# Decode of the second block's weights begun four groups later, the coarse score's third part taken first, and one y operand shifted, in a fused attention and two-block kernel

## The chip, the cores and the metric

The kernel runs on one core of one Trainium2 chip. The metric is the device time of one execution in microseconds, from the chip's own records; lower is better. A change of about 0.5% (4 us) is the least that the measurement of this kernel tells from no change.

## The reference

`setup_inputs` draws 4 batches of 8 heads, 576 positions of 64 elements, all float32. Each head gets two attentions that are added: a coarse one over means of 4 positions (144 by 144 scores), repeated 4 times, and a local one with a band of 7 positions. The sum, as 2304 tokens by 512, goes through two blocks of products.

```python
out_d = sm_attn(q_d, k_d, v_d)            # q, k, v averaged over 4 positions: 144 x 144 scores
out_up = np.repeat(out_d, factor, axis=2)
mask = np.abs(pos[:, None] - pos[None, :]) < factor
...
return (out_up + out_local).astype(np.float32)

def _moe_ref(x, w1, w2, w3, w_out):       # 512 -> 1024 -> 512
    a = x @ w1
    b = x @ w2
    h = a * b @ w3
    return (h @ w_out).astype(np.float32)

def _moe2_ref(x, w_in, w_out):            # 512 -> 2048 -> 512
    h = x @ w_in
    g = h * (1.0 / (1.0 + np.exp(-h)))
    return (g @ w_out).astype(np.float32)
```

## The kernel before

**Work and stages.** One pass over the core's time has four stages. An opening (to about 109 us) loads and decodes the first block's weights and runs the first attention units by a list of names written out by hand. Then come the `ab` products (x by w1 and w2, line 675), 128 *groups* numbered by slot; then the `yb` products (line 1126, from 360 us), the second block's first product `h` (line 1180) and its second `o` (line 1313). Weights arrive as 64-bit numbers and are turned into float32 on the chip: ScalarE scales (line 186, `dec`), VectorE clamps (line 191), shifts the low word (line 197, `sw`) and joins (line 203).

**Order.** From slot 18 on, TensorE's order is fixed by the code; the other engines' orders are set by a scheduler that simulates the program, so that an edit of a start slot moves rows on all of them. Every engine runs its rows in order. So does SP, whose queue issues every DMA, and a DMA that waits holds up those behind it.

**Attention in the background.** The 16 *units* (two heads each) run beside the `ab` groups. TensorE counts a *beat* after every three matmuls (four to a group), and the tables `SUMS` and `TURN` name the beat of each step of a unit u: `td` (transposes of the coarse scores, line 439) and `tl` (of the local ones, line 469), `od` (coarse sums, line 499), `sd` of the next unit (its coarse scores, lines 372 and 377), `s` (its local scores, line 414), and `ol` (local sums, line 521). From `sd` to `ol` lie 8 beats for the pairs 7/6 and 8/7 (`sd7` to `ol6`, `sd8` to `ol7`), and 14 for later ones. After `sd`, VectorE takes maxima (lines 396 and 398, `smd`), a mean of the next unit's q and k (line 321, `qkd`) and the scaled maxima (line 399); ScalarE then takes exponentials (line 339, `Ed` from `sd`, then `band`), GpSimd normalizes (line 356). The result of `ol` goes out as `xf` (VectorE, line 534), a ScalarE cast (line 549) and GpSimd's rest (line 553) to `x`, which the `ab` products of the next batch read.

**Two T banks.** `od`, the third part of a split coarse score (`sd_1`, `other` in the code), both halves of `ol`, `td` and `tl` share two PSUM tiles of tag T, in rotation. The second half of `ol` takes the one that held `sd_1`, so it waits until the exponentials have read the third part. A score is split for units over 5.

**Decode in the background.** `units` of the second block's weights (16, line 760) are loaded by `bg_load` (two DMAs of 512 KB into one of two staging buffers, `sw`), and `bg_steps` puts their decode and four mixes (line 814, `res`) and stores at slots from `starts[n]`:

```python
starts = [22 + (13 * n) // 3 for n in range(len(units))]
at(NSTATIC + 2, lambda: bg_load(0))       # NSTATIC is 18
...
(0, first), (1, clamp), (3, low), (4, lambda: bg_load(n + 2)),
(4, lambda: mix(0)), (5, store_plain), (5, lambda: mix(1)), (6, store_mixed),
```

At `bg_end` = `starts[-1] + 9` the pools of the next stage open and `r_load(0)` reads four blocks of the `ab` results back (`cb`, `cr`, line 960).

**y operands.** Seven tiles of tag `c_` (6 KB a partition) hold the split operands of the `yb` and `h` products, in rotation. After the `h` stage, tiles of the `o` stage (A, S1 to S4) lie where they were.

Of the kernel before, what the change touches and what calls it, by code (L numbers as in the profile page):

```python
# [9 lines left out]
F32R = mybir.dt.float32r  # L10
AF = mybir.ActivationFunctionType
ALU = mybir.AluOpType
AX = mybir.AxisListType

NB, NHP, S, P = 4, 4, 576, 128
# [4 lines left out]
NQB, QW, KW = 9, 32, 38  # L20
# [53 lines left out]
def tile_model(ctx: ExitStack, tc: tile.TileContext, qk, vw, vr, w12, w3t, wo, wb, out):  # L74
    nc = tc.nc
# [69 lines left out]
    for g in range(4):  # L145
        mv = mask[QW * g:QW * g + QW]
        nc.gpsimd.affine_select(
            out=mv, in_=mv, compare_op=ALU.is_ge, fill=NEG, base=0,
# [3 lines left out]
            out=mv, in_=mv, compare_op=ALU.is_ge, fill=NEG, base=6,  # L152
# [13 lines left out]
    def op(name, fn):  # L166
        assert name not in ops, name
        ops[name] = fn
# [11 lines left out]
    def stage(home, name):  # L180
        return home.tile([P, 2, 512, 2], I32, tag="st", name=name, bufs=2)
# [148 lines left out]
    def unit_ops(u):  # L330
        U = str(u)
        hold = {}
# [1 line left out]
        def small(tag):  # L334
            return att.tile([P, 2 * NQB], F32, tag=tag, name=tag)

        def exps(z, src, E, lo, hi, n, scale):
            for j in range(lo, hi):
                nc.scalar.activation(  # L339
                    E[:, j, :], src[j], AF.Exp, bias=z[:, j:j + 1], scale=scale,  # L340
                    accum_out=z[:, NQB + j:NQB + j + 1],
                )
# [8 lines left out]
        def norm(z, E, n, width, lo, hi):  # L351
            if opening[0]:
                for j in range(lo, hi):
                    nc.scalar.mul(E[:, j, :], E[:, j, :], z[:, NQB + j:NQB + j + 1])
            elif lo == 0:
                nc.gpsimd.tensor_tensor(
                    out=E, in0=E, op=ALU.mult,
                    in1=z[:, NQB:NQB + n].unsqueeze(2).to_broadcast([P, n, width]),
                )

        split = u > 5
# [30 lines left out]
        def coarse_max():  # L392
            hold["zd"] = att.tile([P, NQB + 3], F32, tag="smd", name="smd")
            m = hold["zd"][:, 3:6]
            n = 2 if split else 3
            nc.vector.tensor_reduce(out=m[:, :n], in_=hold["pair"], axis=AX.X, op=ALU.max)
            if split:
                nc.vector.tensor_reduce(out=m[:, 2:3], in_=hold["sv"][2], axis=AX.X, op=ALU.max)
            nc.vector.tensor_scalar(
                out=hold["zd"][:, 0:3], in0=m, scalar1=-1.0 / 128.0, scalar2=None, op0=ALU.mult  # L400
            )

        def coarse_exps():
            hold["Ed"] = att.tile([P, 3, SD], F32, tag="Ed", name=f"Ed{u}", bufs=1)
            exps(hold["zd"], hold["sv"], hold["Ed"], 0, 3, 3, 1.0 / 128.0)

        def local_scores():
            t = A["qk", u]
# [12 lines left out]
        EL = band[:, :, 0:KW]  # L421
# [40 lines left out]
        def local_turn(k):  # L462
            c0, c1, w = TL[k]
            flat = band.rearrange("p i k -> p (i k)")
            if k == 0:
                hold["ET"] = att.tile([64 + KW, 5, P], F32, tag="ET", name=f"ET{u}", bufs=1)
            tp = t_tile(f"tl{u}_{c0}")
            for c in range(c0, c1):
                nc.tensor.transpose(
                    tp[:w, (c - c0) * P:(c - c0 + 1) * P], flat[:, 128 * c:128 * c + w], ident,  # L470
                )
            hold["tl", k] = tp

        def local_copy(k):
            c0, c1, w = TL[k]
            mark(nc.scalar.copy(
                hold["ET"][:w, c0:c1, :].rearrange("p c q -> p (c q)"),
                hold["tl", k][:w, :(c1 - c0) * P],
            ))
# [83 lines left out]
        op("mk" + U, local_mask)  # L563
        op("ml" + U, local_max)
        for k in range(3):
            op(f"x{k}" + U, lambda k=k: exps(hold["zl"], [EL[:, j, :] for j in range(NQB)], EL, 3 * k, 3 * k + 3, NQB, 1.0))
            op(f"n{k}" + U, lambda k=k: norm(hold["zl"], EL, NQB, KW, 3 * k, 3 * k + 3))
            op(f"tl{k}" + U, lambda k=k: local_turn(k))
            op(f"cl{k}" + U, lambda k=k: local_copy(k))
# [18 lines left out]
    for u in range(NU):  # L588
        unit_ops(u)
# [71 lines left out]
    NH = 384  # L661
    NT = NTOK // (2 * NH)
# [80 lines left out]
    NSTATIC = 18  # L743
# [16 lines left out]
    units = [(kind, p) for p in range(8) for kind in range(2)]  # L760
    bg = {}

    def bg_load(n):
        if n >= len(units):
            return
        kind, p = units[n]
        if wide:
            st = stage(stg, "sw")
        else:
            st = stg.tile([P, 2, 512], F32, tag="st", name="sw", bufs=2)  # L770
        for t in range(2):
            src = wb[2 * p + kind, :, t * 512:(t + 1) * 512]
            if wide:
                nc.sync.dma_start(st[:, t].rearrange("p n w -> p (n w)"), src.bitcast(I32))
            else:
                nc.sync.dma_start(st[:, t], src)
        bg["st", n] = st
# [57 lines left out]
    def at(slot, fn):  # L835
        plan.setdefault(slot, []).append(fn)

    starts = [22 + (13 * n) // 3 for n in range(len(units))]
    at(NSTATIC + 2, lambda: bg_load(0))
    at(NSTATIC + 5, lambda: bg_load(1))  # L840
    for n in range(len(units)):
        for k, fn in bg_steps(n):
            at(starts[n] + k, fn)
# [1 line left out]

    NUN = 8 * NT
    yp = []
    Y, YC, WC = {}, {}, {}


# [23 lines left out]
    def cx_half(name, dtype):  # L874
        return b3[0].tile([P, 4 * NH], dtype, tag="ch", name=name, bufs=2)

    def y_high(t, i, e=None):
        if i // 2 == 2 * t - 2 and t:
            d = cx_half(f"yc{t}_{i}", F32R).rearrange("p (l k n) -> p l k n", l=2, k=2)
        elif t == 1 and 2 <= i < 4:  # L880
            d = b2[0].tile([P, 2, 8 * P], F32R, tag="a", name=f"yc{t}_{i}", bufs=2)
            d = d[:, :, :2 * NH].rearrange("p l (k n) -> p l k n", k=2)
        else:
            d = yp[0].tile([P, 2, 2, NH], F32R, tag="c_", name=f"yc{t}_{i}", bufs=7)
        if e is None:
            nc.scalar.copy(d[:, 0], Y[t][CH[i][0]])
        else:
            e.tensor_copy(d[:, 0], Y[t][CH[i][0]])
        YC[t, i] = d
# [89 lines left out]
    def r_slot(j, g):  # L979
        name = f"co{j}_{g}"  # L980
        if j == 20:
            return cx_half(name, F32R).rearrange("p (l k n) -> p l k n", l=2, k=2)
        if j == 19 or (j < 14 and (2 * j + g) % 9 > 6):
            d = b2[0].tile([P, 2, 8 * P], F32R, tag="a", name=name, bufs=2)
            return d[:, :, :2 * NH].rearrange("p l (k n) -> p l k n", k=2)
        return yp[0].tile([P, 2, 2, NH], F32R, tag="c_", name=name, bufs=7)

    def r_split(j, g):
        t, i = divmod(j, 7)
# [13 lines left out]
    def w_mix(name):  # L1003
        q = {
            "q0": WQ[0][:, 0], "q3": WQ[0][:, 1], "q1": WQ[1][:, 0], "q2": WQ[1][:, 1],
        }
        if name == "r2":
            v = c_pools[0].tile([P, 4, 256], F32, tag="rw", name="rw", bufs=1)
            nc.vector.tensor_tensor(out=v, in0=q["q3"], in1=q["q2"], op=ALU.add)
            WY["f", 5] = v  # L1010
        elif name == "r3":
            nc.vector.tensor_tensor(out=q["q3"], in0=q["q0"], in1=q["q3"], op=ALU.subtract)
            WY["f", 6] = q["q3"]
        elif name == "r0":
            v = WY["f", 5]
            nc.vector.tensor_tensor(out=v, in0=v, in1=q["q0"], op=ALU.subtract)
            WY["f", 3] = v
        else:
            nc.vector.tensor_tensor(out=q["q1"], in0=q["q1"], in1=WY["f", 3], op=ALU.subtract)
            WY["f", 4] = q["q1"]  # L1020

    def w_split(o):
# [9 lines left out]
    todo = (  # L1032
        (102, lambda: w_mix("r2")), (104, lambda: w_mix("r3")),
        (105, lambda: r_split(0, 0)), (105, lambda: r_split(0, 1)),
        (106, lambda: r_mix(0, "t1")), (107, lambda: r_split(1, 0)), (108, lambda: r_split(1, 1)),
        (110, lambda: r_split(2, 0)), (111, lambda: r_split(2, 1)), (112, lambda: r_mix(0, "t2")),
        (113, lambda: r_split(3, 0)),
        (101, lambda: w_split(0)), (105, lambda: w_split(5)), (107, lambda: w_mix("r0")),
        (109, lambda: w_split(1)), (114, lambda: w_split(3)), (115, lambda: w_mix("r1")),
        (117, lambda: w_split(2)), (121, lambda: w_split(4)), (125, lambda: w_split(6)),  # L1040
# [358 lines left out]
    E = mybir.EngineType  # L1399
    with tc.manual_schedule(engines={E.PE, E.DVE, E.Activation, E.Pool, E.SP}):  # L1400
        for t in range(NT):
# [10 lines left out]
            for i in range(7):  # L1412
                j = 7 * t + i
# [18 lines left out]
        for u in range(NUN):  # L1432
            t, p = divmod(u, 8)
# [5 lines left out]
            if t == 0:  # L1439
                todo = {p_: (2 * p_ + 2, 2 * p_ + 3) for p_ in range(6)}  # L1440
                for k, s in enumerate(todo.get(p, ())):
                    put((1, 3)[k], lambda s=s: wc_high(s), lambda s=s: wc_rest(s, nc.vector))
            if t + 1 < NT:
# [4 lines left out]
                todo = {5: ((4, 0),), 6: ((1, 1), (3, 2), (5, 3)), 7: ((1, 4), (3, 5), (5, 6))}  # L1448
# [83 lines left out]
```

## Time and profile before

| | |
|---|---|
| median of 3 runs | 805.39 us (805.06, 805.39, 808.16) |
| profiled execution, its own time | 804.82 us |
| span in the profile | 803.0 us |
| PE, PEld busy | 99%, 92% of the span |
| DVE, ACT, POOL busy | 71%, 56%, 8% |
| mean granted TensorE clock | 0.997 |

PE is TensorE's matmuls, PEld its weight loads, DVE VectorE, ACT ScalarE, POOL GpSimd, SPq the SP queue that issues DMAs. Busy shares are of the span from first to last instruction; the execution's own time is 1.8 us longer. A granted clock of 1.0 is 2.4 GHz, 0.5 is 1.2 GHz.

### The profile page before, as it was taken

The numbers are of one execution on the slowest core, as the hardware profiler recorded it, in microseconds if no ns is written. First come the engines' busy times: TensorE is split into PE (matmuls) and PEld (weight loads), VectorE is DVE, ScalarE is ACT, GpSimd is POOL, SyncE is SP. The second block draws the span as 40 slices with busy tenths as digits, with TensorE's granted clock in tenths as the row PEclk, the third lists the DMA queues.
The fourth block names the chain that finished last, engine by engine and source line by source line (L and its number), as shares of the span: only waits on it lengthen the run. The fifth ranks groups of instructions, "written<-read, shape, count | busy, mean of one in ns | idle before, by whom it ended". The sixth has DMA issues, their size and how long they took to land.

```text
span 803.0 us, 19022 instructions
## 1 busy us (share of the span) xinstructions
PE 791.6 (99%) x7510; PEld 739.7 (92%) x7510; DVE 569.4 (71%) x870; ACT 445.8 (56%) x1136; POOL 67.5 (8%) x84
## 2 busy tenths in 40 slices
PE   8999999999999999999999999999999999999998
PEld 5555699889999999999999999999999999999998
DVE  7988884867878874836889567445565798777771
ACT  6687864555555552525447577547578654444441
POOL 3000101423332220000000000000000000000000
PEclk9999999999999999999999999999999999999999
DMA  9977774689899887226485663454788955555540
GB/s 312 379 213 250 237 230 136 182 248 297 289 304 312 273 279 257 52 49 235 132 321 152 203 197 99 123 177 115 239 257 239 334 184 190 185 187 185 192 132 27
DMA packets 109353, 168.68 MB, mean 210 GB/s; under 512 B 20176, under 2 KB 80080, under 8 KB 108880
## 3 DMA queue, kind: packets, MB, share of 16 engines
q1 hardware_dynamic: 109264, 167.46, 65.0%
q8 instruction: 59, 0.97, 0.5%
q14 instruction: 30, 0.25, 0.1%
HBM read 115.00 MB, written 52.43 MB: 209 GB/s over the span
## 4 chain that ended last, share of the span: by engine, by line
PE 87%; DMA 5%; DVE 4%; issue 1%; SPq 1%; ACT 1%; POOL 0%; DVEq 0%; ACTq 0%; POOLq 0%
PE ab L675 23%; PE yb L1126 11%; PE ox L1313 10%; PE hx L1180 9%; PE oy L1313 6%; PE hy L1180 6%; PE wp L635 3%; PE oz L1313 3%; PE hv L1180 3%; PE hz L1180 3%; PE ov L1313 3%; PE ol L521 2%; DMA st<-w 2%; DMA vr<-vr 1%; DMA qk<-qk 1%; PE td L439 1%
## 5 line engine op out<-in xcount | busy, mean ns | idle before, releaser
L675 PE MATMUL ab<-x,w_wB 128*128 128x320 f32 (+1 forms) x768 | 109.6, 300 | 0.0
L675 PE MATMUL ab<-x,w_wA 128*128 128x320 f32 (+1 forms) x768 | 107.6, 297 | 1.0 <-DVE w_wA L280 1.0
L675 PEld LDWEIGHTS ab<-x,w_wB 128*128 128x128 f32 x768 | 103.7, 190 | 1.1 <-issue 0.7
L675 PEld LDWEIGHTS ab<-x,w_wA 128*128 128x128 f32 x768 | 102.2, 189 | 1.8 <-DVE w_wA L280 1.3
L1126 PE MATMUL yb<-co,wy 128*128 128x384 f32 x504 | 87.5, 336 | 0.0
L1126 PEld LDWEIGHTS yb<-co,wy 128*128 128x128 f32 x504 | 87.3, 188 | 0.0
L1180 PE MATMUL hx<-yc,wc 128*128 128x384 f32 x432 | 82.9, 336 | 0.0
L1180 PEld LDWEIGHTS hx<-yc,wc 128*128 128x128 f32 x432 | 75.6, 188 | 0.0
L635 PE MATMUL wp<-w_wo,w_w 128*128 128x512 f32 x128 | 60.1, 602 | 0.3 <-DVE w_wo L203 0.2
L1180 PE MATMUL hy<-yc,wc 128*128 128x384 f32 x288 | 57.8, 336 | 0.0
L687 ACT COPY af<-ab 128x320 f32<-128x320 f32 (+1 forms) x64 | 25.1, 396 | 58.5 <-PE ab L675 52.2
L1313 PE MATMUL oy<-wo,S 128*128 128x256 f32 x432 | 53.8, 281 | 0.0
L1313 PE MATMUL ox<-wo,S 128*128 128x256 f32 x432 | 53.8, 281 | 0.0
L1313 PEld LDWEIGHTS oy<-wo,S 128*128 128x128 f32 x432 | 52.2, 189 | 0.0
L1313 PEld LDWEIGHTS ox<-wo,S 128*128 128x128 f32 x432 | 52.2, 189 | 0.0
L1180 PEld LDWEIGHTS hy<-yc,wc 128*128 128x128 f32 x288 | 50.6, 188 | 0.0
L1162 ACT ACTIVATE c<-c 128x384 f32<-128x384 f32 x96 | 48.0, 525 | 3.8 <-DVE c L1092 3.1
L693 DVE TENSOR_TENSOR cf<-ab,af 128x320 f32<-128x320 f32 (+1 forms) x64 | 28.8, 449 | 24.8 <-PE ab L675 11.4
L339 ACT ACTIVATE band<-band,sml 128x38 f32<-128x38 f32 x144 | 44.9, 319 | 2.2 <-DVE sml L430 2.2
L635 PEld LDWEIGHTS wp<-w_wo,w_w 128*128 128x128 f32 x128 | 22.4, 190 | 21.2 <-issue 19.0
L1186 ACT COPY p<-hx 128x384 f32<-128x384 f32 x24 | 11.5, 478 | 44.4 <-PE hx L1180 44.4
L993 DVE TENSOR_TENSOR co<-cb,co 128x768 fp32r<-128x768 f32 x32 | 29.3, 955 | 9.3 <-ACT co L992 8.6
(183 smaller groups left out, 1455.5 us busy)
## 6 DMA issues: line engine op xcount, KB each, us to landing
gd<-c SPq DMA_DIRECT2D x96, 192.0 KB
sw<-wb SPq DMA_DIRECT2D x32, 512.0 KB
qk<-qk SPq DMA_DIRECT2D x16, 579.0 KB
big<-gd SPq DMA_DIRECT2D x18, 512.0 KB
A<-gd SPq DMA_DIRECT2D x18, 512.0 KB
S<-gd SPq DMA_DIRECT2D x17, 512.0 KB
cb<-cd SPq DMA_DIRECT2D x10, 768.0 KB
st<-w SPq DMA_DIRECT2D x14, 512.0 KB
```

The lines of the kernel that those rows point to most:

```text
L339: nc.scalar.activation(E[:, j, :], src[j], AF.Exp, bias=z[:, j:j + 1], scale=scale, accum_out=z[:, NQB + j:NQB + j + 1],)
L521: nc.tensor.matmul(acc[h][r, c0:c0 + QW], lhsT=v[k, sub, c, r], rhs=ET[k, c, q0:q0 + QW], start=True, stop=True,)
L635: nc.tensor.matmul(wp_ps[half, j], lhsT=w3v[:, k, j * P:(j + 1) * P], rhs=wov[:, k, :], start=(gp == 0 and k == 0), stop=(gp == 3 and k == 1),
L675: nc.tensor.matmul(acc[:, :N], lhsT=wv[:, i, w, kk, :], rhs=X[b, h, kk][:, j, :], start=(n == 0), stop=(n == 11),)
L687: mark(nc.scalar.copy(af, C.pop(("ab", b, h, m, 0))[:, :N]))
L693: nc.vector.tensor_tensor(out=cf, in0=C.pop(("ab", b, h, m, 1))[:, :N], in1=C.pop(("af", b, h, m)), op=ALU.mult)
L993: nc.vector.tensor_tensor(out=d[:, 1], in0=src, in1=d[:, 0].bitcast(F32), op=ALU.subtract)
L1126: nc.tensor.matmul(acc[e], lhsT=WY[o][:, a, 2 * g + k, c0:c0 + P], rhs=y[:, b, k, :], start=(n < 2 and (a, b) == (0, 0) and i in (0, 1, 2, ...
L1162: nc.scalar.activation(v, v, AF.Silu)
L1180: nc.tensor.matmul(acc, lhsT=WC[s][:, a, c, kt * P:(kt + 1) * P], rhs=y[:, b, kt, :], start=(n == 0 and i in (0, 1, 2, 4)), stop=(n == 5), ...
L1186: nc.scalar.copy(p1, X_)
L1313: nc.tensor.matmul(acc, lhsT=A[:, a, p * P:(p + 1) * P], rhs=B_[name, p // 4][:, b, p % 4, :], start=(p == 0 and q == 0 and name in begin) ...
```

## The change

Three edits. The background decode starts at slot 26 and steps by 17/4 slots a unit (before: 22 and 13/3), and its first two loads are asked for 3 slots later. For split scores the maximum and the exponential of the third part come first. The tag `c_` becomes seven tags with one buffer each; the fifth is 512 bytes a partition larger, and the last tile's seventh operand lies 192 bytes into it.

```diff
-        def exps(z, src, E, lo, hi, n, scale):
-            for j in range(lo, hi):
+        def exps(z, src, E, todo, scale):
+            for j in todo:
...
-            nc.vector.tensor_reduce(out=m[:, :n], in_=hold["pair"], axis=AX.X, op=ALU.max)
             if split:
                 nc.vector.tensor_reduce(out=m[:, 2:3], in_=hold["sv"][2], axis=AX.X, op=ALU.max)
+            nc.vector.tensor_reduce(out=m[:, :n], in_=hold["pair"], axis=AX.X, op=ALU.max)
...
-            exps(hold["zd"], hold["sv"], hold["Ed"], 0, 3, 3, 1.0 / 128.0)
+            exps(hold["zd"], hold["sv"], hold["Ed"], (2, 0, 1) if split else range(3), 1.0 / 128.0)
...
-    starts = [22 + (13 * n) // 3 for n in range(len(units))]
-    at(NSTATIC + 2, lambda: bg_load(0))
-    at(NSTATIC + 5, lambda: bg_load(1))
+    starts = [26 + (17 * n) // 4 for n in range(len(units))]
+    at(NSTATIC + 5, lambda: bg_load(0))
+    at(NSTATIC + 8, lambda: bg_load(1))
...
+    SHIFTED = 4
+    n_slot = [0]
+    def c_slot(name):
+        k, n_slot[0] = n_slot[0] % 7, n_slot[0] + 1
+        d = yp[0].tile(
+            [P, 4 * NH + (128 if k == SHIFTED else 0)], F32R, tag=f"c_{k}", name=name, bufs=1
+        )
+        c0 = 48 if name == f"yc{NT - 1}_6" else 0
+        return d[:, c0:c0 + 4 * NH].rearrange("p (l k n) -> p l k n", l=2, k=2)
...
-            d = yp[0].tile([P, 2, 2, NH], F32R, tag="c_", name=f"yc{t}_{i}", bufs=7)
+            d = c_slot(f"yc{t}_{i}")
...
-        return yp[0].tile([P, 2, 2, NH], F32R, tag="c_", name=name, bufs=7)
+        return c_slot(name)
```

TensorE's rows stand in the same order as before. On the other engines three places matter.

The first is VectorE around the coarse scores of unit 7 (`ods` copies `od6` out of PSUM, `cf` is the product of an `ab` group). Before, the decode of background unit 0 stands among them:

```order
L191 TENSOR_SCALAR dec<-dec 128x1024
L203 SCALAR_TENSOR_TENSOR dec<-dec,sw 128x1024
L814 TENSOR_TENSOR res<-dec 128x256
L693 TENSOR_TENSOR cf_1_3_1967<-ab_1_3_1_1945,af_1_3_1938 128x256
L814 TENSOR_TENSOR res<-dec 128x256
L814 TENSOR_TENSOR res<-res,dec 128x256
L507 COPY ods_1983<-od_1977 128x144
L814 TENSOR_TENSOR res<-dec,res 128x256
L398 TENSOR_REDUCE smd<-sd_1_1986 128x1
L396 TENSOR_REDUCE smd<-sd_1985 128x2
L321 TENSOR_REDUCE qkd_2166<-qk_1822 128x288
L399 TENSOR_SCALAR smd<-smd 128x3
```

and now:

```order
L693 TENSOR_TENSOR cf_1_3_1960<-ab_1_3_1_1938,af_1_3_1933 128x256
L507 COPY ods_1976<-od_1970 128x144
L397 TENSOR_REDUCE smd<-sd_1_1979 128x1
L398 TENSOR_REDUCE smd<-sd_1978 128x2
L321 TENSOR_REDUCE qkd_2155<-qk_1819 128x288
L399 TENSOR_SCALAR smd<-smd 128x3
```

The two decode rows and four mixes are gone from here. The two maxima stood third part first already.

The second is VectorE around the coarse scores of unit 8 and the sums of unit 7. Before, from the join of background unit 1 on:

```order
L203 SCALAR_TENSOR_TENSOR dec<-dec,sw 128x1024
L693 TENSOR_TENSOR cf_1_5_2199<-ab_1_5_1_2186,af_1_5_2164 128x256
L814 TENSOR_TENSOR res<-dec 128x256 x2
L814 TENSOR_TENSOR res<-dec,res 128x256 x2
L507 COPY ods_2236<-od_2230 128x144
L398 TENSOR_REDUCE smd<-sd_1_2239 128x1
L191 TENSOR_SCALAR dec<-dec 128x1024
L396 TENSOR_REDUCE smd<-sd_2238 128x2
L321 TENSOR_REDUCE qkd_2446<-qk_2056 128x288
L399 TENSOR_SCALAR smd<-smd 128x3
```

Now the same kinds of row stand there for background unit 0 (the `res` before `ods`), and behind `smd` this follows:

```order
L203 SCALAR_TENSOR_TENSOR dec<-dec,sw 128x1024
L349 RECIPROCAL smd<-smd 128x3
L197 TENSOR_SCALAR sw<-sw 128x1024
L814 TENSOR_TENSOR res<-dec 128x256
L534 TENSOR_TENSOR xf_0_2375<-ol_0_2337,ods_2221 128x320
L534 TENSOR_TENSOR xf_1_2380<-ol_1_2338,ods_2221 128x256
```

The row L197, the shift of background unit 2 that needs its load, stands ahead of `xf` of unit 7; before, it stood behind it.

The third is the SP queue at that load. Before, the loads `sw` of unit 2 stood between the stores of `ab` groups 2 and 3; now:

```order
L314 DMA vr_2142<-vr 80x1024
L301 DMA qk_2049<-qk 128x1158
L972 DMA cb_4907<-cd_0_84 128x1536
L308 DMA vw_2136<-vw 40x1280
L715 DMA cd_0_87<-cf_1_4_2075 128x64
L715 DMA cd_0_87<-cf_1_4_2075 128x192
L308 DMA vw_2136<-vw 40x2x512
L715 DMA cd_0_87<-cf_1_5_2185 128x64
L715 DMA cd_0_87<-cf_1_5_2185 128x192
L774 DMA sw<-wb 128x1024 x2
L301 DMA qk_2294<-qk 128x1158
```

The loads follow the store of group 5, and one block `cb` that the next stage needs has come forward by some 140 rows into this stretch. GpSimd's addition of unit 8's values (`vr`, line 483) has moved ahead of its normalization of unit 7's `Ed`. With the shift, one wait is gone: a ScalarE cast of the `o` stage (S2 of the first set) no longer waits for the last `h` products.

## Rows read from the trace of the kernel before

**Rows 1.** Windows: length, then busy us (count) by engine, clock, DMA share, GB/s
```profile
128.10:139.70 11.60, 10.91 (x225) 9.85 (x223) 5.30 (x14) 6.13 (x33) 2.86 (x3) 1.00 0.41 118
139.70:152.40 12.70, 12.32 (x232) 10.97 (x233) 10.21 (x22) 7.48 (x35) 4.39 (x5) 1.00 0.65 190
152.40:165.90 13.50, 11.00 (x224) 9.81 (x224) 12.63 (x23) 7.84 (x31) 5.40 (x5) 1.00 0.56 182
165.90:300.54 134.64, 134.64 (x1969) 127.74 (x1972) 104.96 (x217) 73.00 (x293) 43.03 (x46) 0.99 0.89 288
```
**Rows 2.** Waits of PE, 105 to 170 us: total us, times, longest
```profile
PE ol L521 <- ACT Ed L339: 2.5, 3, 1.9
PE tl L469 <- issue: 0.6, 1, 0.6
```
**Rows 3.** Windows behind the longest wait, columns as in the first group
```profile
166.00:171.00 5.00, 5.00 (x28) 4.96 (x29) 3.31 (x10) 2.41 (x13) 3.26 (x4) 0.66 0.94 265
168.00:169.00 1.00, 1.00 (x5) 1.00 (x5) 1.00 (x6) 0.77 (x2) 0.26 (x1) 0.50 0.80 295
```
**Rows 4.** Timeline of PE: start us, us of each group of instructions
```profile
132.80 0.52 PE L372 MATMUL sd<-qkd 64*128 64x144 f32 x4
...
157.41 0.71 PE L499 MATMUL od<-EdT,vd 72*64 72x144 f32 x8
158.05 0.52 PE L372 MATMUL sd<-qkd 64*128 64x144 f32 x4
...
162.48 0.30 PE L521 MATMUL ol<-ET,vw 38*64 38x32 f32 x4
164.66 1.25 PE L521 MATMUL ol<-ET,vw 38*64 38x32 f32 x68 [1.87 <-ACT Ed L339]
...
171.22 2.00 PE L675 MATMUL ab<-x,w_wB 128*128 128x320 f32 x12
```
**Rows 5.** Timeline of ACT
```profile
152.75 1.15 ACT L186 ACTIVATE dec<-sw 128x1024 f32<-128x1024 f32 x1
...
163.41 0.38 ACT L339 ACTIVATE Ed<-sd,smd 128x144 f32<-128x144 f32 x1 [4.41 <-DVE smd L399]
...
164.13 0.38 ACT L339 ACTIVATE Ed<-sd,smd 128x144 f32<-128x144 f32 x1
```
**Rows 6.** Timeline of DVE
```profile
135.40 0.16 DVE L399 TENSOR_SCALAR smd<-smd 128x3 f32<-128x3 f32 x1
...
154.93 3.09 DVE L203 SCALAR_TENSOR_TENSOR dec<-dec,sw 128x1024 int32<-128x1024 int32 x1
...
160.48 0.30 DVE L507 COPY ods<-od 128x144 f32<-128x144 f32 x1
...
163.14 0.15 DVE L399 TENSOR_SCALAR smd<-smd 128x3 f32<-128x3 f32 x1
...
164.71 1.22 DVE L203 SCALAR_TENSOR_TENSOR dec<-dec,sw 128x1024 int32<-128x1024 int32 x1
...
167.69 0.81 DVE L534 TENSOR_TENSOR xf<-ol,ods 128x320 f32<-128x320 f32 x2
```
**Rows 7.** Timeline of POOL
```profile
154.84 1.27 POOL L483 TENSOR_TENSOR vr<-vr 72x512 f32<-72x512 f32 x1 [0.50 <-DMA vr<-vr]
156.07 2.54 POOL L553 TENSOR_TENSOR x<-xf,x 128x320 fp32r<-128x320 f32 x2
...
168.74 0.90 POOL L553 TENSOR_TENSOR x<-xf,x 128x320 fp32r<-128x320 f32 x1 [1.59 <-ACT x L549]
```
**Rows 8.** Timeline of SPq: loads of background weights
```profile
145.72 0.42 SPq L774 DMA_DIRECT2D sw<-wb  x1
...
164.95 0.86 SPq L774 DMA_DIRECT2D sw<-wb  x2
```
**Rows 9.** Timeline of DVE: the shifts that need those loads
```profile
150.95 0.91 DVE L197 TENSOR_SCALAR sw<-sw 128x1024 int32<-128x1024 int32 x1 [0.71 <-DMA sw<-wb]
...
174.00 0.69 DVE L197 TENSOR_SCALAR sw<-sw 128x1024 int32<-128x1024 int32 x1 [4.69 <-DMA sw<-wb]
```

More of the change, by code (lines that the diff above doesn't have):

```diff
@@ L565, in unit_ops @@
         for k in range(3):
-            op(f"x{k}" + U, lambda k=k: exps(hold["zl"], [EL[:, j, :] for j in range(NQB)], EL, 3 * k, 3 * k + 3, NQB, 1.0))
+            op(f"x{k}" + U, lambda k=k: exps(hold["zl"], [EL[:, j, :] for j in range(NQB)], EL, range(3 * k, 3 * k + 3), 1.0))
             op(f"n{k}" + U, lambda k=k: norm(hold["zl"], EL, NQB, KW, 3 * k, 3 * k + 3))
@@ L875, in cx_half @@
         return b3[0].tile([P, 4 * NH], dtype, tag="ch", name=name, bufs=2)
+    n_slot = [0]
[5 more added lines that the diff above has]
+        c0 = 48 if name == f"yc{NT - 1}_6" else 0
+        assert not c0 or k == SHIFTED
+        return d[:, c0:c0 + 4 * NH].rearrange("p (l k n) -> p l k n", l=2, k=2)
     def y_high(t, i, e=None):
```

## The prediction

> **What bounds the kernel now.** I read the table of the profile first: TensorE (PE) is busy for 99% of a span of 803.0 us, at a mean granted clock of 0.997. A gain can only come from the last per cent of idle time, or from the clock. I then asked for the waits of PE and for windows cut at the points where the change moves rows. Before 128 us the change moves nothing. From 165.90 us to the end of the `ab` products PE is busy for all of 134.64 us, so nothing can be gained there except clock; what can be gained lies between 128 and 166 us [rows 1]. In those three windows, length less busy time is 0.69, 0.38 and 2.50 us of idle PE. The list of waits names its causes: three times the second half of `ol` waits for ScalarE's exponentials (2.5 us, the longest 1.9), and once a `tl` waits for 0.6 us [rows 2]. The third thing is the clock. Behind the longest wait the mean granted clock of five microseconds is 0.66; inside them it is 0.50, which is 1.2 GHz; PE had stood for 1.87 us before that, and its work had run at 2.4 GHz until then [rows 1, 3, 4]. Five microseconds at 0.66 do the work of 3.3, so 1.7 us are lost on top of the wait.
>
> The longest wait, followed back. The second half of `ol` of unit 7 starts at 164.66; its first half ran from 162.48 to 162.78 [rows 4]. It needs the T bank that holds the third part of unit 8's coarse score, and that part's exponential stands last, at 164.13, 0.72 us behind the first of the three at 163.41; that first one had waited 4.41 us for the scaled maxima (VectorE's line 399, at 163.14) [rows 5, 6]. From `sd` to line 399 took 5.09 us here (158.05 to 163.14), but 2.60 us for an earlier unit with no decode rows between (132.80 to 135.40) [rows 4, 6]. So VectorE is 2.49 us late. Most of that was there before `sd` came: `od` of unit 7 was done at 158.12, and its copy `ods` started at 160.48, 2.36 us later [rows 4, 6]. In front of `ods` VectorE had the decode of background unit 1. Its join (line 203) started at 154.93 and took 3.09 us, against 1.22 us for the next one at 164.71; GpSimd ran `vr` and two `x` rows in just that time, 154.84 to 158.61 [rows 6, 7].
>
> **The change part by part.**
>
> *Shifted operand: 0.* It takes from ScalarE one wait, on a cast in the `o` stage. No PE wait there hangs on it, and no instruction is added. If the 192 bytes made a matmul's operand read slower it would show in the `yb` and `o` products; the trace has nothing that suggests it, and nothing in the addresses changes the number of columns.
>
> *Third part first in the maxima: 0.* The order already had it so at the units in question.
>
> *Third part first in the exponentials: the T bank comes free 0.72 us earlier* [rows 5]. No row is added, and the other consumers wait for all three.
>
> *Decode four groups later.* This removes a whole unit's decode from VectorE around `sd` of unit 7, puts unit 0's where unit 1's was (around `sd` of unit 8), and lets GpSimd do `vr` earlier, so that it is no longer beside the join. Window by window:
>
> First window, 0.69: I take no gain. The rows that move stand behind it, except for the exponentials' order, and what that frees of the `ol` wait I expect the `td` behind it to wait for again, since its input comes through a load and GpSimd. Bounds 0 to 0.69.
>
> Second window, 0.38: its `ol` wait is smaller than 0.72, so the new order covers it by itself, and the chain loses six decode rows as well. I take 0.3, bounds 0 to 0.38.
>
> Third window, 0.62 of `tl`: its operand is copied by ScalarE behind the scaling of a background unit (152.75, 1.15 us) [rows 5]. Without it the copies are over 1.15 us earlier, PE arrives 0.3 us earlier: I take 0.5, bounds 0 to 0.62.
>
> Third window, 1.88 of `ol`: if all 2.49 us of lateness went, the bank would be free 2.49 + 0.72 - 1.88 = 1.33 us before PE asks. So 1.33 us of lateness may stay and cost nothing. What will stay: of the 2.36 us, the join's excess (3.09 - 1.22 = 1.87) goes wholly if nothing runs beside it, and by half if the `x` rows still do, so 0.5 to 1.4 us stay; and PE comes up to 0.8 us earlier by the terms above. That makes 0.5 to 2.2 us against 1.33, a wait of 0 to 0.9. I take 0, because the middle, 1.3, just fits. The upper bound is 1.88 - 0.72 = 1.16, with VectorE as late as before.
>
> Clock: without a stop of near 2 us I take it that PE stays at 2.4 GHz, as it does through the first two windows with their shorter stops (clock 1.00) [rows 1]: 1.7 us. Bounds 0 to 1.7.
>
> On the join, the Trainium skill ("SBUF — State Buffer", section "Who interferes with whom") says that a VectorE instruction with two SBUF inputs contends with a GpSimd instruction that reads SBUF, one fully blocking the other; 3.09 beside 1.22 us agrees. By it the join would still wait for one `x` row, and the sum would be worse by that wait only as far as it passes the spare time.
>
> Sum: 0.3 + 0.5 + 1.9 + 1.7 = 4.4 us. The profiled execution took 804.82 us, so it would take 800.4; it lies 0.57 us below the median of 805.39, and 805.39 - 4.4 = **801.0 us**. The most there is to gain is 0.69 + 0.38 + 2.50 + 1.7 = 5.3 us (800.1).
>
> Hidden costs. VectorE, ScalarE and GpSimd keep their number of decode rows, and behind 165.90 they are busy for 78%, 54% and 32% of the time [rows 1]: one more unit (some 7 us of VectorE) fits into 29.7 us of idle VectorE. The stores and loads are the same in all.
>
> **The rivals.**
>
> *A. VectorE stays as late.* Unit 0's decode now stands where unit 1's stood, and the join meets GpSimd again. Then only the 0.72 us count: a wait of 1.16 stays, and the clock falls as before. Gain 0.3 + 0.5 + 0.72 = 1.5: 803.9. For it: the same rows in the same place. Against: `vr` (1.27 us) has left that place [rows 7]. Chance 0.12.
>
> *B. A new wait behind the shift of unit 2.* The shift (line 197) now stands ahead of `xf` of unit 7 and needs a load that the queue issues only behind the store of group 5. That group's product stood right behind the join that ended at 158.02 [rows 6]; I take 157.5 for the issue. `xf` to `x` takes 167.69 to 169.64, 1.95 us [rows 6, 7]. The products that read this `x` begin at 171.22, 5.31 us behind the end of `ol` (165.91) of which 1.7 are lost clock [rows 4], so after the change about 3.6 us behind an `ol` that ends near 164.0: at 167.6. Then `xf` has to start by 165.65, and the shift, 0.91 us with a mix of some 0.4 behind it, by 164.35: 6.85 us after the load is issued. Of two earlier such loads one was shifted 5.23 us after its issue (145.72 to 150.95) and one 9.05 us after (164.95 to 174.00, having waited 4.69) [rows 8, 9]. The first costs nothing; the second makes PE wait 2.2 us, and would bring back some of the clock loss: gain 4.4 - 2.2 = 2.2, or 0.5 with the clock: 803.2 to 804.9. For the quick one: the load of 9.05 us ran in a window with a DMA share of 0.94, the stretch before 165.90 has 0.56 [rows 1, 3]. Chance 0.17.
>
> *C. Slower: DMA becomes the bound.* Each unit's load (two of 512 KB) and stores (896 KB) are 1.97 MB. Put four groups later, one unit's worth more has to pass in the stretch behind 165.90, where the DMA share is 0.89 and 288 GB/s flow [rows 1]: 6.8 us at that rate. Idle are 11% of 134.64, 14.8 us. If more than about half of those can't be used, because the queue stands behind waiting rows, the next stage's reads come late by up to 6.8 us: 801.0 + 6.8 = 807.8. It decides from the point where the later loads of attention data (`qk`, `vw`) land after PE asks for them; PE there waits for nothing now, and the units start wider apart than they land. Chance 0.06.
>
> *D. The clock falls all the same,* or by a new short stop elsewhere: the waits go, 2.7 us, and the 1.7 stay lost: 802.7. Chance 0.13.
>
> *E. The change doesn't do what it says:* another row comes to stand in VectorE's way, and less than 0.5 us is gained: 805.0. Chance 0.04.
>
> **How the numbers follow.** The forecast, at 0.48, has its own range from 800.1 (all idle time gone) to 801.9 (the join's lateness costs 0.9). A to E take the other 0.52. The range has to reach over the forecast, D, A and the cheaper half of B: 800.0 to 803.9 holds about 0.8. A measurement of this kernel tells about 0.5% from no change, 4.03 us, so faster means below 801.36. Of the forecast's 0.48 some two thirds lie below it, with a little from the first window's bound; I give 0.42. Slower by over 0.5% is C: 0.05. The rest, 0.53, is within.
>
> **What the new profile would show.** Right: the list of PE waits between 128 and 170 us has no `ol` over 0.3 us and a granted clock of 1.00 in every window behind it; the join beside unit 8 takes under 2.3 us and `ods` starts within 1.5 us of `od`; the first window's idle time stays near 0.7. A: `ol` of unit 7 waits about 1.2 us and the clock shows 0.50 again. B: line 197 waits for `sw` with over 1.3 us ahead of `xf` of unit 7, and an `ab` group waits for `x`. C: the DMA share behind 165 us rises to near 1 and PE waits for a DMA at the last units or at the start of `yb`. D: no wait and a clock below 1. Matmuls of the `yb` stage longer than before would say that the shifted operand isn't free. I would be wrong above all by a stop on PE of under 2 us that still lowers the clock, or by a wait that I have not named, in the 134.64 us that have none now.

## The result, and the profile after

Ten executions of the changed kernel have a median of 799.61 us (795.6 to 805.17), ten of the kernel before 806.75 us (805.06 to 808.16): ratio 0.9915, 95% interval 0.9889 to 0.9942. That is faster, by 7 us where 4.4 were forecast, and 0.4 us below the range. The profiled execution took 797.45 us with a span of 795.7, against 803.0.

The waits of TensorE after, from 105 to 170 us (columns as in [rows 2]):

```profile
PE td L439 <- POOL Ed L356: 1.0, 1, 1.0
PE td L439 <- DVE xf L534: 0.5, 1, 0.5
PE ab L675 <- DVE w_wA L280: 0.3, 1, 0.3
```

And from 170 to 335 us, where it had none before:

```profile
PE ab L675 <- ACT af L687: 1.5, 1, 1.5
PE ab L675 <- issue: 0.9, 1, 0.9
```

The windows of [rows 1] and [rows 3], after:

```profile
128.10:139.70 11.60, 11.15 (x228) 10.19 (x227) 5.35 (x13) 5.75 (x31) 2.42 (x3) 1.00 0.42 131
139.70:152.40 12.70, 12.19 (x235) 11.05 (x235) 5.84 (x17) 7.83 (x40) 5.59 (x7) 1.00 0.50 174
152.40:165.90 13.50, 13.05 (x241) 12.16 (x241) 11.90 (x24) 8.74 (x38) 5.38 (x5) 1.00 0.66 206
165.90:300.54 134.64, 132.25 (x2021) 125.04 (x2020) 101.75 (x216) 72.51 (x284) 44.01 (x45) 1.00 0.87 290
166.00:171.00 5.00, 5.00 (x38) 4.77 (x37) 3.75 (x10) 3.24 (x10) 3.83 (x4) 1.00 0.84 288
```

The forecast's place looks as forecast: the third window lost 2.05 us of its 2.50 us of idle TensorE, no `ol` waits, and the clock behind it is 1.00 where it was 0.66. But the fourth window, which had no idle time, now has 2.39. VectorE's rows around unit 8 (those of [rows 6]), after:

```profile
154.07 1.78 DVE L203 SCALAR_TENSOR_TENSOR dec<-dec,sw 128x1024 int32<-128x1024 int32 x1
158.53 0.29 DVE L507 COPY ods<-od 128x144 f32<-128x144 f32 x1
161.19 0.15 DVE L399 TENSOR_SCALAR smd<-smd 128x3 f32<-128x3 f32 x1
165.17 0.70 DVE L197 TENSOR_SCALAR sw<-sw 128x1024 int32<-128x1024 int32 x1 [1.13 <-DMA sw<-wb]
166.12 0.82 DVE L534 TENSOR_TENSOR xf<-ol,ods 128x320 f32<-128x320 f32 x2
```

The join takes 1.78 us in place of 3.09, and the shift ahead of `xf` waits 1.13 us for its load, just under the 1.3 that the forecast named for rival B.

All this gives little: the `ab` products, from the first start to the last, take 263.1 us (94.8 to 357.9) where they took 265.7 (93.6 to 359.3), 2.6 us less, and they begin 1.2 us later. The rest of the 7.3 us lies where the forecast had put 0. The list of groups shows two of the `o` stage's, before and then after (busy us, mean ns of one, idle us):

```profile
L1313 PE MATMUL oy<-wo,S 128*128 128x256 f32 x432 | 53.8, 281 | 0.0
L1313 PE MATMUL ox<-wo,S 128*128 128x256 f32 x432 | 53.8, 281 | 0.0
```
```profile
L1325 PE MATMUL oy<-wo,S 128*128 128x256 f32 x432 | 52.1, 277 | 0.0
L1325 PE MATMUL ox<-wo,S 128*128 128x256 f32 x432 | 51.9, 276 | 0.0
```

Nothing waited there in either, and the clock is the same. The timeline shows it as a spacing. Before, 24 products begin every 2.83 us, 117.8 ns each:

```profile
630.00 2.99 PE L1313 MATMUL oy<-wo,S 128*128 128x256 f32 x24
632.83 2.99 PE L1313 MATMUL ox<-wo,S 128*128 128x256 f32 x24
635.66 2.99 PE L1313 MATMUL oy<-wo,S 128*128 128x256 f32 x24
```

After, every 2.72 us, 113.3 ns each, but for two short holds, by the starts of single products 0.20 us at 634.08 (shown) and 0.31 us at 653.44:

```profile
628.55 2.88 PE L1325 MATMUL oy<-wo,S 128*128 128x256 f32 x24
631.27 2.88 PE L1325 MATMUL ox<-wo,S 128*128 128x256 f32 x24
634.08 3.00 PE L1325 MATMUL oy<-wo,S 128*128 128x256 f32 x24
636.92 2.88 PE L1325 MATMUL ox<-wo,S 128*128 128x256 f32 x24
```

Over 1512 products from first to last that is 177.96 us before and 171.80 after: 6.2 of the 7.3 us.

The weight loads show the same two states. One view of `oy`'s loads, of the kernel before and of e1_shift (below), which has no hold (min, median and max ns of one, first and last start):

```profile
L1313 PEld LDWEIGHTS oy<-wo,S x432: 187/188/193, 629.9 to 796.5; 128*128 128x128 f32 x144
```
```profile
L1325 PEld LDWEIGHTS oy<-wo,S x432: 187/188/188, 633.2 to 793.6; 128*128 128x128 f32 x144
```

Of the stage's 1512 loads one in three takes 191 to 193 ns before and none over 188 in e1_shift; wherever a profile of this study shows the long spacing its loads do the former, wherever the short one the latter.

### The profile page after: what moved, and what is told of

It reads as the page before. It is cut to its first block, busy times and chain, and to the rows that moved or that the text cites. A ratio compares the mean times of both kernels' runs of the same rounds, so it can differ in the third digit from the quotient of the medians.

```text
span 795.7 us, 19018 instructions
## 1 busy us (share of the span) xinstructions
PE 783.7 (98%) x7510; PEld 731.2 (92%) x7510; DVE 562.6 (71%) x870; ACT 446.9 (56%) x1136; POOL 69.4 (9%) x84
## 4 chain that ended last, share of the span: by engine, by line
PE 85%; DMA 9%; DVE 2%; ACT 2%; issue 1%; SPq 1%; POOL 0%; ACTq 0%; DVEq 0%; POOLq 0%
PE ab L675 21%; PE yb L1138 11%; PE ox L1325 10%; PE hx L1192 9%; PE hy L1192 6%; PE oy L1325 6%; PE hv L1192 3%; PE hz L1192 3%; PE oz L1325 3%; PE wp L635 3%; PE ov L1325 3%; PE ol L521 2%; DMA st<-w 2%; DMA lent<-w3t 2%; DMA lent<-wo 2%; DMA vw<-vw 2%
## 5 line engine op out<-in xcount | busy, mean ns | idle before, releaser
L1325 PE MATMUL oy<-wo,S 128*128 128x256 f32 x432 | 52.1, 277 | 0.0
L1325 PE MATMUL ox<-wo,S 128*128 128x256 f32 x432 | 51.9, 276 | 0.0
L1325 PEld LDWEIGHTS oy<-wo,S 128*128 128x128 f32 x432 | 50.3, 188 | 0.4 <-ACT p5o L1336 0.2
L1325 PEld LDWEIGHTS ox<-wo,S 128*128 128x128 f32 x432 | 50.3, 188 | 0.0
L1198 ACT COPY p<-hx 128x384 f32<-128x384 f32 x24 | 11.5, 480 | 44.0 <-PE hx L1192 44.0
L1004 ACT CAST co<-cb 128x768 fp32r<-128x768 f32 x32 | 25.7, 836 | 17.8 <-DVE cb L988 14.3
```

Source lines behind the costliest of these rows:

```text
L1004: nc.scalar.copy(d[:, 0], src)
L1198: nc.scalar.copy(p1, X_)
L1325: nc.tensor.matmul(acc, lhsT=A[:, a, p * P:(p + 1) * P], rhs=B_[name, p // 4][:, b, p % 4, :], start=(p == 0 and q == 0 and name in begin) ...
```

## The experiments

In what follows a *set* is one of the nine of the `o` stage, 168 products. Ratios are to executions of the kernel before on the same chip.

**One part of the change at a time.** `e1_shift` is the kernel before with the new `c_slot` alone, `e2_noshift` the changed kernel with the old tag `c_` of seven buffers, and the other two have one edit of the diff each. Of e1_shift's edit, one of the two places that use `c_slot`:

```diff
...
-            d = yp[0].tile([P, 2, 2, NH], F32R, tag="c_", name=f"yc{t}_{i}", bufs=7)
+            d = c_slot(f"yc{t}_{i}")
...
```

> Shift of the y operands alone. In the profile after, 6.2 of the 7.3 us that the span lost lie in the o stage, whose 1512 products follow one another at 113.3 ns and not 117.8. Theory S (the shift, by new places of the y operands, lets TensorE keep the shorter spacing): about 6 us less than before, o products at 113 ns in the profile, and the 1.9 us wait of ol still there; some 799 to 801 us. Theory R (the spacing is a matter of when the products of a stage begin against each other, and the edits of the ab stage changed that): spacing and time as before, 805 to 807 us.

> Later weights and the third part first, without the shift. Theory S: the ab stage is 1.4 us shorter as in the profile after, the o products stay at 117.8 ns, 804 to 805.5 us. Theory R: o products at 113 ns in most executions, and the time of the whole change, 797 to 802 us.

> Later weights alone. By the forecast's terms the chain behind unit 8's scores is no longer late by more than the wait, so the ol wait of unit 7 goes nearly all (under 0.5 us) without the new order of the exponentials, and the clock stays at 1.00 behind it: end of the ab products 1 to 2 us earlier than before. Theory S: 804 to 805.5 us, theory R: o products at 113 ns and 797 to 802 us.

> Third part first alone. By the forecast's terms the wait of ol in unit 7 falls from 1.88 by 0.72 to some 1.2 us; whether the clock still falls to 0.50 behind a wait of that length is open: if it does, 0.7 to 1 us is gained in the ab stage, if not some 2.5. With the o products at 117.8 ns that is 803.5 to 806 us in all.

Measured: e1_shift 0.9958 (0.9933 to 0.9984), e2_noshift 1.0006 (0.9984 to 1.0029), e3_starts 0.9979 (0.9957 to 1.0001), e4_exps 1.0004 (0.9983 to 1.0024). In the profiles the `o` stage took 171.27 us in e1_shift and 177.96 in the three without the shift, as before. Theory S held: the shift alone shortens the stage, by 6.7 us. The edits of the `ab` stage bring nothing that these executions can tell, together or alone, though each does its work: the longest `ol` wait was 0.7 us in e3_starts and 1.0 in e4_exps, and e2_noshift has none over 0.3.

Why e1_shift is only 3.4 us faster by its ratio, and not 6.7, shows in its opening and in those of others. A window of each from its opening, e1_shift, e4_exps and e8_step (below):

```profile
24.00:26.00 2.00, 2.00 (x69) 1.56 (x60) 1.97 (x3) 0.37 (x1) 0.00 (x0) 0.50 1.01 404
```
```profile
25.00:31.00 6.00, 6.00 (x25) 3.42 (x26) 5.19 (x11) 3.17 (x12) 0.00 (x0) 0.50 1.05 388
```
```profile
23.00:32.00 9.00, 8.78 (x101) 5.48 (x102) 7.31 (x13) 3.88 (x13) 0.00 (x0) 0.50 1.03 372
```

The granted clock falls to 0.50 (1.2 GHz) there in some profiles and in others not, in rows that no edit touches; the first `ab` product comes at 93.6 to 99.8 us. What that costs shows in the mean granted clock of each execution: e1_shift's twelve go from 796.79 us at 1.000 to 804.24 at 0.991. With 800 us x (1 - clock) taken off each time, an estimate of what the lower clock cost, the medians are 797.1 us for e1_shift and 803.7 for the kernel before beside it, 6.6 apart: the whole of what the stage lost in the profile. A stage that no hold or clock disturbs agrees between profiles to 0.1 us; totals of a dozen executions as they stand only to some 2.

**What in the shift does it.** `e5_tags` sets `c0 = 0`, `e7_other` gives the 192 bytes to another operand, `e6_nudge` is the kernel before with one small product more:

```diff
+            if n == 0 and k == 0:
+                nc.tensor.matmul(
+                    acc[:, :64], lhsT=A[:, 0, :P], rhs=B_[name, 0][:, 0, 0, :64],
+                    start=True, stop=True, skip_group_check=True,
+                )
```

> The shift alone without its 192 bytes: seven tags, the fifth 512 bytes larger, the last operand at the tile's start. The shift alone gave o products at 113.3 ns, and its own 48 products on the shifted operand ran unevenly at 176 ns where all others take 173.3. Theory P (the uneven products just ahead of the o stage put TensorE into the shorter spacing): products on the last operand even at 173.3, o products at 117.8 ns. Theory T (the new places of the tiles do it): o products at 113.3 ns.

> The kernel before with one product of 64 columns more, on the operands of the first o product and into the bank that this one clears, just ahead of the o stage; its result is never read. Theory P (the o stage keeps the spacing in which it is entered, whatever disturbs the entry): o products at 113.3 ns, o stage 6.5 us shorter, 798.5 to 799.5 us on a median of 805.5. Theory Q (it must be the uneven products on the shifted operand): 117.8 ns, and no change, 805 to 806 us.

> The shift alone, but the 192 bytes given to the fourth operand of the last tile (the fourth tag is the larger one), of which 48 products run three groups of 48 ahead of the last ones of the last unit. Theory P: these products run unevenly, the ones behind them are even again, and the o stage is entered from an even group: 117.8 ns. If once disturbed TensorE keeps to the short spacing for good, 113.3 ns.

The last six products of the `h` stage, on the shifted operand in e1_shift and in its old place in e2_noshift (min, median and max ns of one, first and last start):

```profile
L1192 PE MATMUL hx<-yc,wc x6: 333/338/346, 624.1 to 625.0; 128*128 128x384 f32 x6
```
```profile
L1180 PE MATMUL hx<-yc,wc x6: 336/336/339, 618.2 to 619.1; 128*128 128x384 f32 x6
```

The shifted operand makes its products uneven. e7_other (807.02 us, one execution) has them too, but further ahead of the `o` stage, and runs all nine sets at 117.8 ns; e6_nudge as well, 1.0001 (0.9979 to 1.0022), so a small odd product does not do it. e5_tags (798.98 us, one execution) has none, enters at 117.8 ns, and then does something that neither of its two theories foresaw:

```profile
632.33 2.99 PE L1325 MATMUL ox<-wo,S 128*128 128x256 f32 x24
635.90 3.01 PE L1325 MATMUL oy<-wo,S 128*128 128x256 f32 x24 [0.58 <-ACT p5o L1336]
638.75 2.88 PE L1325 MATMUL ox<-wo,S 128*128 128x256 f32 x24
641.47 2.88 PE L1325 MATMUL ox<-wo,A 128*128 128x256 f32 x24
```

TensorE waits 0.58 us, and from there on runs at 113.3 ns to the end. So the addresses are not what carries the short spacing: the `o` operands lie where they lay, and both spacings occur on them. Nor is it the wait that the shift takes from ScalarE: the second `S<-tt_o` cast starts 5.1 us behind the first `o` product before, in e1_shift and in e5_tags alike.

**A stop instead of the shift.** Theory P2 followed: two spacings, each kept until TensorE is disturbed. `e9_stop4` stops it ahead of the fifth set in the kernel before, `e11_stop1` ahead of the second in e2_noshift:

```diff
+        if n == 4:
+            nc.tensor.matmul(
+                X_[:, :64], lhsT=A_[n, "A11"][:, 0, :P], rhs=B_["A11", 0][:, 0, 0, :64],
+                start=True, stop=True, skip_group_check=True,
+            )
+            nc.scalar.copy(p1[:, :64], X_[:, :64])
```

> The kernel before with a stop of TensorE in the middle of the o stage: ahead of the fifth of nine sets one product of 64 columns, whose result ScalarE copies away before the set may begin. Nothing else is changed, and the copy is never read. Theory P2 (two spacings, each of which lasts until TensorE is stopped by a real wait, behind which it runs in the short one): the four sets ahead of the stop at 117.8 ns, the five behind it at 113.3 ns, o stage 840 x 4.4 ns = 3.7 us shorter less the stop. Theory A (the shorter spacing needs the shifted operand): all nine at 117.8 ns.

> Later weights and the third part first without the shift, and the same stop ahead of the second set of the o stage. Theory P2: first set at 117.8 ns, the eight behind at 113.3 ns, 1344 x 4.4 ns = 6.0 us less the stop of some 0.5 to 1.5 us; 799 to 801.5 us, as fast within 2 us as the whole change. Theory A: all at 117.8 ns, 805 to 807 us.

The timeline of e9_stop4 around the stop:

```profile
696.14 2.99 PE L1319 MATMUL oy<-wo,S 128*128 128x256 f32 x24
698.97 2.99 PE L1319 MATMUL ox<-wo,S 128*128 128x256 f32 x24
701.80 0.19 PE L1304 MATMUL ox<-wo,A 128*128 128x64 f32 x1
702.35 3.01 PE L1319 MATMUL ox<-wo,A 128*128 128x256 f32 x24 [0.36 <-ACT p1o L1308]
705.20 2.88 PE L1319 MATMUL oz<-wo,A 128*128 128x256 f32 x24
707.91 2.88 PE L1319 MATMUL ov<-wo,big 128*128 128x256 f32 x24
```

Four sets at 117.8 ns, five at 113.3, in one execution of a kernel with none of the three edits. The stage took 174.91 us. e11_stop1: 0.9948 (0.9923 to 0.9973); its stop of 2.13 us was longer than wished and brought the clock to 0.50 behind it, so that its time is just above the 799 to 801.5 us expected, but all sets behind the second ran at 113.3 ns (stage 176.04 us).

**What makes executions of the changed kernel differ.** It was run again, and in two variants of its `starts`: 26 with step 13/3 (`e8_step`) and 24 with step 13/3 (`e10_start24`, whose first two loads are also asked for 2 slots earlier; its edit of `starts` is shown).

```diff
-    starts = [26 + (17 * n) // 4 for n in range(len(units))]
+    starts = [24 + (13 * n) // 3 for n in range(len(units))]
```

> The whole change with the old step of 13/3 slots a unit and the new first slot of 26. In the profile after, two new waits of TensorE (1.5 and 0.9 us, at 247 and 282 us) stand where exponentials and copies of ScalarE come late behind VectorE's decode rows. Theory: they come of the step, which moves the decode against the attention units; with the old step at least the first goes, 0 to 2 us less than the whole change. If they come of the later start alone, they stay.

> The whole change with first slot 24 and step 13/3, between before and after: the decode of unit 0 then stands between the places that it had in both. If two slots are enough to take it out of the way of unit 8's scores, the ol wait of unit 7 stays away and the two later waits of 1.5 and 0.9 us with the step of 17/4 go: up to 2 us less than the whole change, 797 to 800 us. If not, the ol wait comes back with 1 us or more: 800 to 803 us.

> The changed kernel as it is, beside the others on one chip: o products at 113.3 ns, no ol wait over 0.3 us between 128 and 170 us, two waits of 1 to 1.5 us between 240 and 285 us; 797 to 802 us with the spread that the clock in the opening gives.

e8_step 0.9923 (0.9895 to 0.9952): the wait for `af` was 0.5 in place of 1.5 us and the other gone, but its `ab` products took 263.5 us, no less than the 263.1 of the whole change: at 116 us, well ahead of the waits that the edits move, it waited 1.6 us for the first block's weights (`w_wA`), where the changed kernel waited 0.3. e10_start24 0.9903 (0.987 to 0.9937): neither later wait, but a `td` wait of 1.7 us. There the wait moved with the decode. e12_after 0.9917 (0.9882 to 0.9952), and its profile shows what the first one did not:

```profile
630.38 2.88 PE L1325 MATMUL ox<-wo,S 128*128 128x256 f32 x24
633.10 3.05 PE L1325 MATMUL oy<-wo,S 128*128 128x256 f32 x24
635.99 2.99 PE L1325 MATMUL ox<-wo,S 128*128 128x256 f32 x24
```

The same kernel leaves the short spacing at 633.10 and runs at 117.8 ns to the end: stage 177.51 us, 5.7 more than in the first profile. At this place the products of S4 need the bank that ScalarE's copy `p5o` reads, and the copy stands behind the split of a weight block:

```profile
631.68 1.05 ACT L915 CAST wo<-wo 128x1024 fp32r<-128x1024 f32 x1
632.64 0.37 ACT L1336 COPY p5o<-oy 128x256 f32<-128x256 f32 x1
```

At 113.3 ns TensorE arrives there at the very time when the copy ends, at 633.0. The next kernels move that split behind the copy (`e13_b12`), also with the earlier start (`e14_b12_start24`) and once more (`e15_b12_again`):

```diff
-            2: ("this b12",),
-            3: ("this b13", "next big"),
+            3: ("this b12", "this b13", "next big"),
```

> The whole change, with the split of the thirteenth weight block of the o stage put behind the copy p5o instead of ahead of it on ScalarE (one row moved, in the first set alone). In one profile of the changed kernel the o products left the spacing of 113.3 ns for 117.8 where the products of S4 came 0.06 us before their bank was free, held by that copy; in another they met a longer stop there and kept it. Theory F (this near miss is what makes executions of the changed kernel differ by up to 6 us in the o stage): with the copy a microsecond earlier TensorE meets no wait there, all nine sets run at 113.3 ns, and the median is 1 to 3 us below that of the changed kernel (0.9915 of before): 0.988 to 0.991. Theory N (it falls out of the spacing by chance anywhere): no better than the changed kernel.

> The kernel of e13_b12 once more, for a second profile. Theory F: again nine sets at 113.3 ns and no wait at S4 of the first set. Theory N: one set or more at 117.8 ns in one of the two profiles.

> The same with first slot 24 and step 13/3, which alone gave 0.9903 of before. Theory F: all nine sets at 113.3 ns, 0.985 to 0.99 of before.

e13_b12 0.9925 (0.9894 to 0.9956): no wait in the first set, but the same hold one set later, behind another split:

```profile
652.00 2.88 PE L1325 MATMUL ox<-wo,S 128*128 128x256 f32 x24
654.72 3.06 PE L1325 MATMUL oy<-wo,S 128*128 128x256 f32 x24
657.62 2.99 PE L1325 MATMUL ox<-wo,S 128*128 128x256 f32 x24
```

Its twin e15_b12_again (801.74 us, one execution) was held there too and kept 113.3 ns. e14_b12_start24, which met no hold, 0.9877 (0.9846 to 0.9908), stage 171.27 us. The last two move that second split as well, `next a11` from step 2 to step 3 of the second set:

> The kernel of e13_b12 with one more row moved: in the second set of the o stage the split of the next A11 stands behind the copy p5o on ScalarE instead of ahead of it. e13_b12 passed S4 of the first set without a wait and left the spacing of 113.3 ns at S4 of the second, held there for 0.08 us by the same copy behind that split. Theory F (small holds at just these two places): no wait at either, nine sets at 113.3 ns, 0.987 to 0.990 of before. Theory N (chance anywhere): some executions still at 117.8 ns from another place on, 0.991 to 0.994.

> The same on top of first slot 24 and step 13/3: theory F 0.985 to 0.988 of before and the lowest spread of all, theory N as e14_b12_start24 (0.9877) or above.

e16_both 0.988 (0.9848 to 0.9913), nine sets at 113.3 ns. e17_both_start24 0.9906 (0.9871 to 0.9941), and against theory F its profile has 117.8 ns from the first S4 on:

```profile
632.57 2.88 PE L1325 MATMUL ox<-wo,S 128*128 128x256 f32 x24
635.90 0.38 PE L1325 MATMUL oy<-wo,S 128*128 128x256 f32 x1 [0.45 <-ACT p5o L1336]
636.62 2.98 PE L1325 MATMUL oy<-wo,S 128*128 128x256 f32 x23 [0.34 <-DVE S L1104]
639.43 2.99 PE L1325 MATMUL ox<-wo,S 128*128 128x256 f32 x24
```

Two stops one behind the other, the operand itself late this time. So a stop can lead into either spacing. e14_b12_start24 and e16_both are the fastest kernels of this study; their intervals overlap that of the whole change, so that they beat it isn't shown. But the holds do go with the spread of executions: with the clock's cost taken off as above, the five shifted kernels whose profile met no hold in the `o` stage spread over 2.5 to 6.7 us each (e1_shift 3.9), the four with several executions whose profile was held there (the changed kernel, e12_after, e13_b12, e17_both_start24) over 9.1 to 11.5.

## Why the prediction was wrong

**The shifted operand, forecast at 0: 6.2 us in the profile.** This is the step that failed. It rests on "A gain can only come from the last per cent of idle time, or from the clock": busy time was taken as time that can't shrink. I looked for a wait that it takes away and for products that it slows, found neither, and took the spacing of the `o` products as given. (The place was wrong too: the shifted operand is read by 48 products of the `h` stage, not in `yb` or `o`.) It isn't given: without the shift all of e2_noshift, e3_starts, e4_exps and the kernel before ran the stage at 117.8 ns, with it e1_shift at 113.3. The 192 bytes make the last products of the `h` stage uneven, just ahead of a stage of 1512 like products that keeps what it is entered with until a hold. Shown: that the spacing is a state (e9_stop4 has both), that the uneven products just ahead of the stage go with the short one (all ten profiles of kernels that have them there enter it at 113.3 ns; e5_tags, e7_other and all without the shift enter it at 117.8; e5_tags differs from e1_shift by the 192 bytes alone), and that holds can end or begin it. Only argued: that unevenness as such is the cause. Open: which holds lead into which. By the starts of single products, 0.06 us of hold ended the short spacing in e12_after and 0.08 us in e13_b12, 0.16 us left it standing in e15_b12_again, 0.20 and 0.31 us in the first profile of the changed kernel, waits of 0.36 and 0.58 us began it in e9_stop4 and e5_tags; but waits of 0.45 and 0.34 us behind one another ended it in e17_both_start24, which fits no rule of length.

**The idle time in the three windows: right in kind.** Forecast 0, 0.3 and 2.4 us; measured 0.24, -0.13 and 2.05, together 2.16 of 2.7. The first window's `td` wait grew, to 0.96, since it waits for GpSimd's `Ed` as said; it straddles the border, and its 0.51 us behind 139.70 are all that the second window has left, whose `ol` wait went. The third has left 0.45 us of a `td` that waits for `xf`. From `sd` to line 399 it took 3.84 us (157.35 to 161.19), 1.24 more than the 2.60 of the unit with no decode rows between, where 1.33 could be spared.

**The clock, 1.7 us: right in the profile, not a sure thing.** The clock stayed at 1.00 behind unit 7 in the changed kernel. But e6_nudge, with the old order and an `ol` wait of 2.0 us, kept 1.00 too:

```profile
167.00:172.00 5.00, 5.00 (x45) 4.93 (x40) 3.56 (x11) 3.47 (x18) 3.00 (x4) 1.00 0.84 269
```

and e11_stop1, which has the new `starts`, fell to 0.50 behind its new wait of 1.49 us at 248:

```profile
250.00:256.00 6.00, 6.00 (x51) 5.94 (x48) 3.03 (x6) 1.19 (x3) 3.95 (x5) 0.50 0.49 173
```

So 1.7 us is what one execution lost. Of six profiled kernels with the old `starts` and the old exponentials five fell between 150 and 175 us.

**"A wait that I have not named, in the 134.64 us that have none": it came, 2.39 us.** With the new `starts`, ScalarE's copy `af` at 247 stands behind a unit's exponentials and the scaling of a background unit, and TensorE waits 1.5 us for the bank that it frees; before, it stood ahead of those exponentials. The copy before, and then after:

```profile
246.47 0.43 ACT L687 COPY af<-ab 128x320 f32<-128x320 f32 x1 [3.72 <-PE ab L675]
```
```profile
247.27 0.74 ACT L687 COPY af<-ab 128x320 f32<-128x320 f32 x2
```

The sum forecast for the `ab` stage, 4.4 us, is the second term that failed: it came out at 2.6 in the profile, and between 1.3 us gained and 2.3 lost in e2_noshift's interval. Over all profiles the `ab` products, first start to last, take 264.1 to 267.1 us in the six kernels with the old `starts` and exponentials (mean 265.6) and 263.1 to 266.4 in the seven with both edits (mean 264.6): some 1 us, less than the profiles of like kernels differ by. The new wait of 1.5 us stands in e2_noshift too; that it is what eats the gain there is likely but not shown.

**Luck.** That the whole came within 3 us of the forecast is luck: the terms that were added up brought next to nothing in the executions, and the one put at 0 brought nearly all.

**The rivals.** A fell: `ol` waits for nothing. B came to 1.13 us on VectorE and cost TensorE nothing there. C fell: the DMA share of the long window went from 0.89 to 0.87. D: not in the changed kernel's profiles, but in e11_stop1 and e15_b12_again. E fell for the change as a whole; for the edits that it speaks of, less than 0.5 us gained lies inside e2_noshift's interval.

## What to carry to other kernels

Where one stage repeats the same product a thousand times, work out its spacing from the starts in the timeline (2.83 or 2.72 us for 24) and not only its waits: 4.4 ns a product were worth more here than every wait of the attention units, and no view of waits shows them. Such a spacing may be a state of the engine that a hold of under 0.1 us ends, so look where an engine that got faster arrives just as its bank is freed. And when an edit only moves background work, ask which later unit stands where the first one stood.

## What the runs showed of the hardware

Products of 128x256 on the same operands ran at 113.3 or 117.8 ns apart at a granted clock of 1.00, each for over 170 us without a break (171.27 us in e1_shift, 177.96 before), and went from one to the other only at a hold. At 117.8 ns one weight load in three took 191 to 193 ns, at 113.3 none over 188. Products of 128x384 kept 173.3 ns in all of this, but those whose moving operand lay 192 bytes further were 176 apart on the mean of 48 in e1_shift. The granted clock halved behind some waits of 1 to 2 us (1.05 us in e4_exps, 1.87 before) and not behind others (1.5 us in the changed kernel, 2.02 in e6_nudge), and in the opening of some profiles and not of others; executions of e1_shift at a mean clock of 0.991 and 1.000 differ by some 7 us.
